# A chunked DeltaNet with a SiLU feed-forward: readout rows of even and odd heads exchanged, recurrence steps paired anew across the quarters of TensorE

## The chip, the cores and the metric

The kernel runs on one core of a Trainium2 chip. A core has five engines that run their own instruction queues side by side: TensorE (PE, matrix products from SBUF into PSUM), VectorE (DVE), ScalarE (ACT), GpSimd (POOL) and SyncE (SP, which here issues nearly all DMAs). The metric is the device time of one execution in microseconds.

PSUM has eight banks, and the kernel divides them into three rooms: three banks for room A, three for room CC, two for room M. A product of small matrices uses a part of TensorE's array: the rows of the array belong to the partitions that its operands lie on, the columns to the partitions that its result goes to. A product with 64 partitions on either side uses one quarter of the array. Write LO for partitions 0 to 63 and HI for 64 to 127. The quarters (from LO to LO) and (from HI to HI) are the main diagonal; (LO to HI) and (HI to LO) are the other diagonal.

## The reference

For 4 batches and 8 heads, over 768 tokens of width 48, a state of 48 x 48 numbers per head is carried from token to token; the output of all heads of a token, side by side, is a row of 384 numbers, which a feed-forward layer takes on.

```python
k_n = k / (np.linalg.norm(k, axis=-1, keepdims=True) + 1e-06)
for t in range(S):
    y[:, :, t] = np.einsum('bhd,bhde->bhe', q[:, :, t], state)
    v_old = np.einsum('bhde,bhd->bhe', state, k_n[:, :, t])
    state = state + beta_t * np.einsum('bhd,bhe->bhde', k_n[:, :, t], v[:, :, t] - v_old)
x = y.transpose(0, 2, 1, 3).reshape(4 * 768, 8 * 48)
h = x @ w_in                 # 384 -> 2048
out = (h * sigmoid(h)) @ w_out   # 2048 -> 384
```

Everything is float32, except that the feed-forward weights arrive as pairs of 32-bit words and are narrowed on the chip.

## The kernel before

The 768 tokens are cut into six chunks of 128 (`c` from 0 to 5), each of two halves of 64 (`hf`). Inside a half the recurrence over tokens is solved at once with the inverse of a triangular 64 x 64 matrix per head, so that only the states go from half to half. The batches form two groups of two (`g`), and each group has 16 heads (2 batches `u`, 4 pairs `p`, and `e`, 0 for the even head of a pair and 1 for the odd one).

`prepare(c)` makes the products of keys with keys and of queries with keys, `invert(c)` inverts the 32 x 32 blocks of the triangular matrices on VectorE and sends them through DRAM to where they are wanted, and `solve(c)` is the recurrence. Its steps are short groups of small products:

- `merge(c, g, second)` (L651) makes the lower left 32 x 32 blocks of the inverses out of the diagonal ones, 32 products of 32 x 32; the second pass multiplies what the first has left in `y`. ACT copies one half of the result (L659, L656) and DVE the other (L660, L657), one behind the other.
- `keys(c, g, hf)` (L676) is what the state gives for the keys, 16 products of 48 x 64 by 48; DVE adds it to `vf` (L681).
- `inner(c, g, hf)` (L688) multiplies `vf` by the inverse, 16 products; ACT copies the result to `zbuf` (L454).
- `update(c, g, hf)` (L708) makes the change of the state out of `zbuf`, 16 products; DVE adds it to the state (L713).
- `old(c, g, hf)` (L749) and `new(c, g, hf)` (L762), 16 products each, add into one PSUM bank the readout of the queries from the state and from `zbuf`. ACT copies the odd heads' rows to `part` (L770), from which five DMAs on SP's queue put them where they belong in `xT`; ACT and DVE in turn copy the even heads' rows straight into `xT` (L454, L457).

Each of these 16 products lies on one quarter, and even and odd heads use the two quarters of one diagonal: with `hf` 0, all of them the main diagonal; with `hf` 1, `keys`, `update` and `new` the other diagonal, `inner` and `old` the main one.

`together(a, b)` issues one product of `a`, one of `b`, and so on in turn. `made(c, g, hf)` is `update` and behind it `new`. The feed-forward is `hidden` (L848: `phid`, full-array products with 256 columns, whose SiLU ACT makes) and, from chunk 1 on, `combine` (L945: chains of full-array products with 192 columns, over sums that DVE makes, `sum_g`, L928). It is cut into pieces, and the loop over the chunks sets by hand how many pieces stand behind each step of the recurrence (`run(n)`), and how many of the squares and norms of the next chunk's keys are issued with them (`go(long, n)`; POOL squares, L328, DVE adds, L332, and the norm steps L346 to L373). The pieces next to a recurrence step come from the chunk before; from the seventh step on `hidden` of the same chunk begins, which reads `xT`.

`pin` keeps the order on each engine as it is written. TensorE's queue is therefore one line of recurrence steps and feed-forward pieces in turn.

Of the kernel before, what the change touches and what calls it, by code (L numbers as in the profile page):

```python
# [21 lines left out]
def kernel(  # L22
# [10 lines left out]
    nc = tc.nc  # L33
    B, H, S, D = q.shape
    DM, DFF = moe_w_in.shape
    P = 128
# [600 lines left out]
    def merge(c, g, second):  # L637

        if c not in ys:
            ys[c] = work.tile([P, 2, HH, T], FP32, name="y", tag="g", bufs=1)  # L640
        y = ys[c]
        pm = bank(A, "px" if second else "py")
        for n in range(HH):
            for k in range(2):
                even, odd = slice(W * k, W * k + T), slice(W * k + T, W * (k + 1))
                if second:
                    to, left, right = even, y[odd, g, n, :], xis[g][odd, n, T:W]
                else:
                    left = aps[c, g][even, 0, n // H, n % H, T:W]
                    to, right = odd, xes[c][even, g * HH + n, :]  # L650
                pin(nc.tensor.matmul(  # L651
                    pm[to, T * n : T * (n + 1)], lhsT=left, rhs=right, start=True, stop=True
                ))
        pm = pm[:].rearrange("p (h t) -> p h t", h=HH)
        if second:
            pin(nc.scalar.copy(xis[g][0:T, :, T:W], pm[0:T]))  # L656
            pin(nc.vector.tensor_copy(out=xis[g][W : W + T, :, T:W], in_=pm[W : W + T]))  # L657
        else:
            pin(nc.scalar.copy(y[T:W, g], pm[T:W]))  # L659
            pin(nc.vector.tensor_copy(out=y[W + T : P, g], in_=pm[W + T : P]))  # L660

    def of_heads():

        for u in range(HB):
            for p in range(NP):
                for e in range(2):
                    yield u, p, e, u * NP + p, slice(W * e, W * e + D), HALVES[e]
# [4 lines left out]
    def keys(c, g, hf):  # L672

        ph = bank(CC, "ph")
        for u, p, e, n, of, _ in of_heads():
            yield pin(nc.tensor.matmul(  # L676
                ph[on(e, hf), n * D : (n + 1) * D], lhsT=kqs[c, g * HB + u][of, p, 0, on(e, hf)],
                rhs=states[g][of, u, p, 0:D], start=True, stop=True,
            ))
        to = vfs[c][:, hf, g * HB : (g + 1) * HB]  # L680
        pin(nc.vector.tensor_tensor(out=to, in0=to, in1=by_heads(ph), op=ALU.add))  # L681
# [19 lines left out]
    def update(c, g, hf):  # L701

        if c == NCH - 1 and hf == 1:
            return
        pu = bank(CC, "pu")
        for u, p, e, n, _, to in of_heads():
            rows = on(e, hf)
            yield pin(nc.tensor.matmul(  # L708
                pu[to, n * D : (n + 1) * D], lhsT=kbufs[c % 2][rows, g * HB + u, p, e, :],
                rhs=zbuf[rows, g * HB + u, hf, p, 0:D], start=True, stop=True,  # L710
            ))
        to = states[g][:, :, :, 0:D]
        pin(nc.vector.tensor_tensor(out=to, in0=to, in1=by_heads(pu), op=ALU.add))  # L713
# [31 lines left out]
    def old(c, g, hf):  # L745

        py = pys[g] = bank(A, "pyc")
        for u, p, e, _, of, to in of_heads():
            yield pin(nc.tensor.matmul(  # L749
                py[to, C * p + W * u : C * p + W * (u + 1)],  # L750
                lhsT=states[g][of, u, p, :], rhs=kqs[c, g * HB + u][of, p, 1, on(e, hf)],
                start=p == 0 and u == 0, stop=False, skip_group_check=True,
            ))
        if hf == 1:
            by_act(read[:], py[:, 0 : 512 : W])

    def new(c, g, hf):

        py = pys.pop(g)
        for u, p, e, _, _, to in of_heads():  # L760
            rows = on(e, hf)
            yield pin(nc.tensor.matmul(  # L762
                py[to, C * p + W * u : C * p + W * (u + 1)], lhsT=zbuf[rows, g * HB + u, hf, p, :],
                rhs=aps[c, g][rows, 1, u, 2 * p + e, :], start=False, stop=True, skip_group_check=True,
            ))
        xT, half = x_half(c, g, hf)
        if g == 0:
            parts[c, hf] = work.tile([P, 2, NP, C], FP32, name="part", tag="x", bufs=1)
        part = parts[c, hf][:, g]
        pin(nc.scalar.copy(part[W : W + D], py[W : W + D].rearrange("p (a t) -> p a t", a=NP)))  # L770
        turns = 0
        for h in chained(range(1, H, 2), range(0, H, 2)):
            f = D * h
            while f < D * (h + 1):
                n, at = min(D * (h + 1) - f, P - f % P), W * (h % 2) + f - D * h
                while h % 2 == 0 and (n > T and at % W or f % P % W and n > T):
                    n = T
                to = xT[f % P : f % P + n, f // P, half]
                if h % 2 == 1:
                    in_line(nc.sync.dma_start(out=to, in_=part[at : at + n, h // 2, :]))  # L780
                else:
                    (by_dve if turns % 2 else by_act)(to, py[at : at + n, C * (h // 2) : C * (h // 2 + 1)])
                    turns += 1
                f += n

    def made(c, g, hf):

        together(update(c, g, hf))
        together(new(c, g, hf))
        if hf == 1 and g == 1:  # L790
            load_q(c + 1)

    def solve(c):

        if c == 0:
            merge(0, 0, False)
            merge(0, 1, False)
            yield
            merge(0, 0, True)
            merge(0, 1, True)  # L800
            yield
            together(inner(0, 0, 0, CC))
            together(inner(0, 1, 0, M))
            yield
            first_outputs(0)
            yield
            first_outputs(1)
            yield
            together(update(0, 0, 0), update(0, 1, 0))
            yield  # L810
            together(keys(0, 0, 1))
            yield
        else:
            for second in (False, True):
                for g in range(2):
                    merge(c, g, second)
                yield
            together(keys(c, 0, 0))
            yield
            together(keys(c, 1, 0), inner(c, 0, 0))  # L820
            yield
            together(inner(c, 1, 0), old(c, 0, 0))
            made(c, 0, 0)
            yield
# [406 lines left out]
    go(long, 99)  # L1231
    load_v(1)
# [82 lines left out]
```

## Time and profile before

| | |
|---|---|
| time, median of 3 runs | 743.81 us (740.95 to 746.01) |
| profiled execution | 745.45 us |
| its span, first to last instruction | 743.7 us |
| mean granted TensorE clock | 0.973 |
| PE busy | 713.0 us, 96% |
| DVE busy | 392.7 us, 53% |
| ACT busy | 204.5 us, 27% |
| POOL busy | 82.1 us, 11% |
| DMA queue 1 | 47.63 MB, 32.6% of 16 engines |

The profile lists instructions by source line, engine and tile. `L688 PE MATMUL pz<-vf,xi 64*64 64x48` is a product issued at line 688 that writes tile `pz`, on a part of the array with 64 rows and 64 columns, with 64 x 48 moving numbers; each product of the program stands in it as two records. PE's records overlap, as products are pipelined, so that a step's time is read from its first start to the start of what comes next. The page cuts the span into 40 slices, and gives in tenths how busy each engine was and what clock TensorE was granted; the same can be asked for any stretch of time. A chunk takes some 111 us, and its recurrence about 40 us of them, feed-forward pieces included.

### The profile page before, as it was taken

The numbers are of one execution on the slowest core, as the hardware profiler recorded it, in microseconds if no ns is written. First come the engines' busy times: TensorE is split into PE (matmuls) and PEld (weight loads), VectorE is DVE, ScalarE is ACT, GpSimd is POOL, SyncE is SP. The second block draws the span as 40 slices with busy tenths as digits, with TensorE's granted clock in tenths as the row PEclk, the third lists the DMA queues.
The fourth block names the chain that finished last, engine by engine and source line by source line (L and its number), as shares of the span: only waits on it lengthen the run. The fifth ranks groups of instructions, "written<-read, shape, count | busy, mean of one in ns | idle before, by whom it ended". The sixth has DMA issues, their size and how long they took to land. (4 is left out here: it accounts for less than half of the span.)

```text
span 743.7 us, 21255 instructions
## 1 busy us (share of the span) xinstructions
PE 713.0 (96%) x9416; PEld 616.8 (83%) x9416; DVE 392.7 (53%) x930; ACT 204.5 (27%) x429; POOL 82.1 (11%) x86
## 2 busy tenths in 40 slices
PE   7869988899989999999999999999999999999996
PEld 5557875486778989988989988989988989989996
DVE  5755588995442693542693542693543692321112
ACT  3523556122223113223113223113223113231120
POOL 4041426300002000002000001000001000000000
PEclk9865999999999999999999999999999999999999
DMA  8754368404017504017404017504017104010000
GB/s 121 210 119 130 130 147 204 74 5 97 11 27 100 86 22 87 8 40 100 86 22 86 10 43 96 86 22 86 10 45 95 42 22 87 11 36 1 22 0 22
DMA packets 149132, 49.25 MB, mean 66 GB/s; under 512 B 134881, under 2 KB 142177, under 8 KB 149041
## 3 DMA queue, kind: packets, MB, share of 16 engines
q1 hardware_dynamic: 146928, 47.63, 32.6%
q8 instruction: 74, 1.21, 0.7%
q10 hardware_dynamic: 2112, 0.26, 0.3%
q14 instruction: 18, 0.14, 0.1%
HBM read 33.91 MB, written 11.80 MB: 61 GB/s over the span
## 5 line engine op out<-in xcount | busy, mean ns | idle before, releaser
L848 PE MATMUL phid<-xT,w_in 128*128 128x256 f32 x1152 | 263.6, 383 | 2.8 <-DVE n L361 0.7
L848 PEld LDWEIGHTS phid<-xT,w_in 128*128 128x128 f32 x1152 | 214.0, 190 | 37.0 <-DVE o L953 2.9
L858 ACT ACTIVATE gT<-phid 128x512 f32<-128x512 f32 x96 | 57.3, 597 | 179.4 <-PE phid L848 163.5
L514 DVE SCALAR_TENSOR_TENSOR rank<-g,step,x 128x31 f32<-128x31 f32 (+15 forms) x155 | 62.2, 402 | 14.3 <-DMA g<-blocks 9.8
L928 DVE TENSOR_TENSOR sums_of_g<-gT 128x384 f32<-128x384 f32 (+1 forms) x60 | 29.3, 510 | 68.2 <-ACT gT L858 57.8
L519 DVE TENSOR_TENSOR x<-x,rank 128x31 f32<-128x31 f32 (+15 forms) x155 | 54.7, 353 | 5.8
L945 PE MATMUL px<-sums_of_w,sums_of_g 128*128 128x192 f32 x320 | 57.2, 330 | 0.0
L945 PE MATMUL py<-w_out,sums_of_g 128*128 128x192 f32 x320 | 56.9, 329 | 0.0
L945 PEld LDWEIGHTS px<-sums_of_w,sums_of_g 128*128 128x128 f32 x320 | 52.0, 190 | 0.8
L945 PEld LDWEIGHTS py<-w_out,sums_of_g 128*128 128x128 f32 x320 | 52.2, 190 | 0.5 <-issue 0.2
L878 PE MATMUL po<-w_out,gT 128*128 128x384 f32 x128 | 45.5, 498 | 2.9 <-POOL w_out L199 2.9
L328 POOL TENSOR_TENSOR sq<-kb 128x384 f32<-128x384 f32 x24 | 19.5, 835 | 237.6 <-PE px L651 219.3
L688 PEld LDWEIGHTS pz<-vf,xi 64*64 64x64 f32 x768 | 41.0, 144 | 5.2 <-issue 2.9
L688 PE MATMUL pz<-vf,xi 64*64 64x48 f32 x768 | 43.9, 227 | 0.3
L457 DVE COPY xT<-pyc 32x128 f32<-32x128 f32 (+2 forms) x66 | 18.7, 284 | 47.3 <-ACT xT L454 47.3
L449 DVE TENSOR_TENSOR ap<-pa,above 128x256 f32<-128x256 f32 x40 | 15.1, 420 | 50.9 <-ACT ap L454 39.0
L878 PEld LDWEIGHTS po<-w_out,gT 128*128 128x128 f32 x128 | 23.1, 189 | 19.8 <-POOL w_out L199 6.0
L749 PE MATMUL pyc<-kq,state 48*64 48x64 f32 x704 | 36.3, 227 | 0.0
L749 PEld LDWEIGHTS pyc<-kq,state 48*64 48x64 f32 x704 | 33.3, 138 | 3.4 <-issue 3.4
L439 PE MATMUL pa<-kq 48*64 48x128 f32 (+1 forms) x896 | 27.6, 264 | 4.9 <-ACT kq L423 4.6
L713 DVE TENSOR_TENSOR state<-state,pu 128x384 f32<-128x384 f32 x22 | 12.1, 553 | 36.3 <-PE pu L708 36.2
L439 PEld LDWEIGHTS pa<-kq 48*64 48x64 f32 x896 | 21.9, 136 | 11.1 <-ACT kq L423 6.5
(159 smaller groups left out, 920.0 us busy)
## 6 DMA issues: line engine op xcount, KB each, us to landing
vf<-in_v_dram SPq DMA_DIRECT2D x24, 192.0 KB, 5.3
out_dram<-o SPq DMA_DIRECT2D x48, 96.0 KB, 2.2
sums_of_w<-in_moe_w_out_dram SPq DMA_DIRECT2D x5, 768.0 KB, 6.2
w_out<-in_moe_w_in_dram SPq DMA_DIRECT2D x4, 768.0 KB, 4.7
blocks<-ap SPq DMA_DIRECT2D x44, 64.0 KB, 1.9
g<-blocks SPq DMA_DIRECT2D x5, 512.0 KB, 3.7
up<-x SPq DMA_DIRECT2D x5, 512.0 KB, 4.0
xi<-up SPq DMA_DIRECT2D x40, 64.0 KB, 2.6
```

The costliest lines, as they stand in the source:

```text
L328: pin(nc.gpsimd.tensor_tensor(out=squared[c, b // HB][:, b % HB], in0=kb, in1=kb, op=ALU.mult))
L439: pin(nc.tensor.matmul(pa[e][half, p * n * W : (p + 1) * n * W], lhsT=kq[rows, p, 0, half], rhs=kq[rows, p, js[0] : js[-1] + 1, half], sta ...
L457: return pin(nc.vector.tensor_copy(out=to, in_=of))
L514: pin(nc.vector.scalar_tensor_tensor(out=tv, in0=g[:, 0:m, m : m + 1].to_broadcast([P, m, n]), scalar=step[:, m : m + 1], in1=x[:, m : m + ...
L519: yield pin(nc.vector.tensor_tensor(out=x[:, 0:m, m:T], in0=x[:, 0:m, m:T], in1=tv, op=ALU.add))
L688: yield pin(nc.tensor.matmul(pz[rows, n * D : (n + 1) * D], lhsT=xis[g][rows, u * H + 2 * p + e, :], rhs=vfs[c][rows, hf, g * HB + u, p, : ...
L749: yield pin(nc.tensor.matmul(py[to, C * p + W * u : C * p + W * (u + 1)], lhsT=states[g][of, u, p, :], rhs=kqs[c, g * HB + u][of, p, 1, on ...
L848: pin(nc.tensor.matmul(ph[:, j * GT : (j + 1) * GT], lhsT=w_in[:, a, (2 * f + j) * P : (2 * f + j + 1) * P], rhs=xTs[c, hf][:, a, :], star ...
L858: pin(nc.scalar.activation(out=gTs[f // FG][:, f % FG, :], in_=ph[:], func=ACTF.Silu, scale=0.5))
L878: pin(nc.tensor.matmul(po[n][:, 0:DM], lhsT=gTs[f // 2 // FG][:, f // 2 % FG, at : at + C], rhs=w_outs[f // HFF][:, f % HFF, :], start=(f ...
L928: pin(nc.vector.tensor_tensor(out=sums_of_g[:, k, fs], in0=of[0], in1=of[1], op=op))
L945: pin(nc.tensor.matmul(to, lhsT=at, rhs=quarter(f, *b) if isinstance(b, tuple) else sums_of_w[b][:, f], start=start and f == 0, stop=f == ...
```

## The change

Three things change.

1. `old` and `new` put the even heads' readout on the upper half of the PSUM bank and the odd heads' on the lower half, where it was the other way round. Both products so move to the other diagonal than before. The copies and DMAs that take the bank's rows to `xT` follow.
2. `merge` becomes a generator that yields before each pair of products, so that it can be issued in turn with another step.
3. In chunks 1 to 5 the steps of `solve` are paired anew, twelve steps in place of nine; `made` issues `update` and `new` in turn. In chunk 0 the second half of the steps changes in the same way. The loops that place feed-forward pieces and norm steps behind the recurrence steps are counted anew.

```diff
@@ merge
         for n in range(HH):
             for k in range(2):
+                if k == 0:
+                    yield
@@ old (and new in the same way)
-                py[to, C * p + W * u : C * p + W * (u + 1)],
+                py[HALVES[1 - e], C * p + W * u : C * p + W * (u + 1)],
@@ new
-        pin(nc.scalar.copy(part[W : W + D], py[W : W + D].rearrange("p (a t) -> p a t", a=NP)))
+        pin(nc.scalar.copy(part[0:D], py[0:D].rearrange("p (a t) -> p a t", a=NP)))
@@ made
-        together(update(c, g, hf))
-        together(new(c, g, hf))
+        together(update(c, g, hf), new(c, g, hf))
@@ solve, chunks 1 to 5
-            for second in (False, True):
-                for g in range(2):
-                    merge(c, g, second)
-                yield
-            together(keys(c, 0, 0))
-            yield
-            together(keys(c, 1, 0), inner(c, 0, 0))
-            yield
-            together(inner(c, 1, 0), old(c, 0, 0))
+            together(merge(c, 0, False))
+            yield
+            together(merge(c, 1, False), merge(c, 0, True))
+            yield
+            together(merge(c, 1, True), keys(c, 0, 0))
+            yield
+            together(keys(c, 1, 0), old(c, 0, 0))
+            yield
+            together(inner(c, 0, 0), old(c, 1, 0))
+            yield
             made(c, 0, 0)
             yield
-            together(old(c, 1, 0), keys(c, 0, 1))
+            together(inner(c, 1, 0), keys(c, 0, 1))
+            yield
             made(c, 1, 0)
             yield
@@ solve, all chunks
-        together(keys(c, 1, 1), inner(c, 0, 1))
-        yield
-        together(inner(c, 1, 1), old(c, 0, 1))
+        together(inner(c, 0, 1), keys(c, 1, 1), old(c, 0, 1))
+        yield
+        together(inner(c, 1, 1), old(c, 1, 1))
+        yield
         made(c, 0, 1)
         yield
-        together(old(c, 1, 1))
         made(c, 1, 1)
         yield
@@ chunk 0
-    for n in range(5):
+    for n in range(6):
         go(solving)
-        run(2)
+        run((2, 1, 1, 2, 2, 2)[n])
...
-        fill(2)
-        go(long, (0, 1, 1, 4, 6)[n])
+        fill((2, 2, 2, 2, 1, 1)[n])
+        go(long, (0, 1, 1, 4, 3, 3)[n])
@@ chunks 1 to 5
-        for n in range(6):
+        for n in range(8):
             go(solving)
-            run(2 if n in (2, 3) else 1)
-            if n >= 2:
+            run(2 if n == 7 else 1)
+            if n >= 3:
                 go(long, 4)
...
-        for n in range(3):
+        for n in range(4):
             go(solving)
             run()
```

The numbers of instructions of each kind, and of DMAs, stay the same.

More of the change, by code (lines that the diff above doesn't have):

```diff
@@ L747, in old @@
         py = pys[g] = bank(A, "pyc")
-        for u, p, e, _, of, to in of_heads():
+        for u, p, e, _, of, _ in of_heads():
             yield pin(nc.tensor.matmul(
-                py[to, C * p + W * u : C * p + W * (u + 1)],
+                py[HALVES[1 - e], C * p + W * u : C * p + W * (u + 1)],
                 lhsT=states[g][of, u, p, :], rhs=kqs[c, g * HB + u][of, p, 1, on(e, hf)],
@@ L759, in new @@
         py = pys.pop(g)
-        for u, p, e, _, _, to in of_heads():
+        for u, p, e, _, _, _ in of_heads():
             rows = on(e, hf)
             yield pin(nc.tensor.matmul(
-                py[to, C * p + W * u : C * p + W * (u + 1)], lhsT=zbuf[rows, g * HB + u, hf, p, :],
+                py[HALVES[1 - e], C * p + W * u : C * p + W * (u + 1)], lhsT=zbuf[rows, g * HB + u, hf, p, :],
                 rhs=aps[c, g][rows, 1, u, 2 * p + e, :], start=False, stop=True, skip_group_check=True,
@@ L774, in new @@
             while f < D * (h + 1):
-                n, at = min(D * (h + 1) - f, P - f % P), W * (h % 2) + f - D * h
+                n, at = min(D * (h + 1) - f, P - f % P), W * (1 - h % 2) + f - D * h
                 while h % 2 == 0 and (n > T and at % W or f % P % W and n > T):
@@ L795, in solve @@
         if c == 0:
-            merge(0, 0, False)
-            merge(0, 1, False)
-            yield
-            merge(0, 0, True)
-            merge(0, 1, True)
-            yield
+            for second in (False, True):
+                for g in range(2):
+                    together(merge(0, g, second))
+                yield
             together(inner(0, 0, 0, CC))
```

## The prediction

> **What bounds the kernel now.** I read the page's parts 1 and 2 first, then who TensorE waits for, then its order of time in one chunk.
>
> ```profile
> span 743.7 us, 21255 instructions
> ...
> PE 713.0 (96%) x9416; PEld 616.8 (83%) x9416; DVE 392.7 (53%) x930; ACT 204.5 (27%) x429; POOL 82.1 (11%) x86
> ...
> PEclk9865999999999999999999999999999999999999
> ```
>
> TensorE (PE) is busy almost throughout; no other engine is near it. From 100 to 660 us its waits add up to some 11 us; the longest two groups are below (us in total, times, longest), both in the first quarter.
>
> ```profile
> PE po L878 <- POOL w_out L199: 2.9, 5, 0.7
> PE pt L413 <- DMA z<-in_q_dram: 2.4, 2, 2.1
> ```
>
> So from chunk 1 on the time is what PE spends, and an edit is worth the PE time it removes. Chunk 2's recurrence runs from 289.9 to 329.1 us. Its order of time (start, length, group; a product of the program stands as two records):
>
> ```profile
> 289.89 2.21 PE L651 MATMUL py<-xe,ap 32*32 32x32 f32 x128
> 292.03 1.57 PE L945 MATMUL py<-w_out,sums_of_g 128*128 128x192 f32 x8
> 293.53 2.21 PE L651 MATMUL px<-xi,y 32*32 32x32 f32 x128
> 295.67 1.57 PE L945 MATMUL py<-w_out,sums_of_g 128*128 128x192 f32 x8
> 297.17 1.14 PE L676 MATMUL ph<-state,kq 48*64 48x48 f32 x32
> ```
>
> ```profile
> 307.78 1.13 PE L708 MATMUL pu<-z,kb 64*64 64x48 f32 x32
> 308.70 1.16 PE L762 MATMUL pyc<-ap,z 64*64 64x64 f32 x32
> 309.79 1.57 PE L945 MATMUL px<-sums_of_w,sums_of_g 128*128 128x192 f32 x8
> 311.29 0.27 PE L749 MATMUL pyc<-kq,state 48*64 48x64 f32 x1
> ...
> 312.27 1.09 PE L708 MATMUL pu<-z,kb 64*64 64x48 f32 x32
> ```
>
> Lengths overlap, so I count from start to start.
>
> **Rates.** One diagonal (two quarters): 32 `pu` records take 308.70 - 307.78 = 0.92 us, 29 ns each; `pyc<-ap,z`, with 64 columns, 1.09. Both diagonals: `old` and `keys(1,0,1)`, 64 records from 311.29 to 312.27, 0.98 us, 15 ns each. Before the change `keys(1,0,0)` with `inner(0,0)`, both on one diagonal, take 301.03 to 303.06, 2.03 us. So a pair that moves onto both diagonals halves. For 32x32 tiles, 128 records on two tiles take 2.14 us; four tiles at once are seen at 33.10 to 34.29 (L584, 128 records, 1.19 us), though with 16 columns, not 32.
>
> **Chunk 2 before.** The nine recurrence steps, start to the next wide group: 2.14, 2.14, 1.07, 2.03, 3.93, 2.95, 1.07, 3.78, 2.78 = 21.9 us.
>
> **After, without the last merge.** Four pairs (`keys`+`old`, `inner`+`old` twice, `inner`+`keys`) at 1.08 = 4.3. Four `update`+`new` at 1.17 (set by `new`: 1.09 and a remainder) = 4.7; before they took 0.92 + 1.09 each. The step of three has one product on the main diagonal and two on the other: 64 records there at 30 ns, 2.1. `merge(0,F)` alone 1.1; `merge(1,F)` with `merge(0,T)`, four tiles, 1.15. Together 13.35.
>
> **The last merge with `keys(0,0)`: the term that decides.** In the rebuilt order each of the 16 `keys` products (64x64) alternates with two 32x32 products, on the same quarters. Nothing overlaps, so at the least it costs both parts as now, 2.1 us. The trace has no change between 32x32 and 64x64; the nearest rows are changes to and from the full array:
>
> ```profile
> 300.78 0.33 PE L945 MATMUL px<-sums_of_w,sums_of_g 128*128 128x192 f32 x1
> 301.03 0.33 PE L676 MATMUL ph<-state,kq 48*64 48x48 f32 x4
> ```
>
> A 128x192 product normally follows in 0.163 us (2.60 for 16 in the chain); here 0.255, so 0.09 more. It is 0.09 at all full-clock changes without a wait, to 32x32 and 64x64 alike. From the last small record to the first wide one it is 0.121 (32x32) and 0.148 (64x64), where records of one quarter follow in 0.03 and 0.06. If 32 to 64 costs the same, a round is 0.121 + 0.094 (the first pair of records after a change) + 0.148 + 0.059 (four merge records) = 0.42 us, and 16 rounds 6.75 us. I take 6.75, the end all nearby rows point to; the other end, 2.1, stays for a rival.
>
> The Trainium skill, TensorEngine Tiling (Array Packing), section Key Properties, says that a change of tiling mode drains TensorE, and speaks against this step. By that rule it is 6.75 too; no row here shows 32 against 64.
>
> **Other terms per chunk.** Three more steps, so three more pairs of changes: +0.28 (0.09 each; the other half is in the step lengths). Waits: DVE now has `S4` (1.36 us), four `add_squares` that wait for POOL (its second pair starts only after the first is summed) and the first norm steps ahead of the state's addition (0.55); counted in us from the end of the last merge, DVE is through with `vf` at 2.0 and 3.0, `S4` at 4.4, the squares at 7.7, the norm steps at 8.75, the state at 9.3. `keys(0,1)` wants it at 8.9, so +0.4, and all PE work queues behind. `merge(0,T)` wants `y` 1.5 us after its products, and the ACT copy (0.58) and DVE copy (0.70) in turn need 1.6: +0.1. A present wait of 0.17 at 320.9 goes. Waits in all +0.35 net, bounds 0 and 1. The readout copies and DMAs only exchange rows: same counts, same queue order on SP; `xT`'s last DMA landed 5.0 us after `made(1,0)`, and the first `phid` still comes 4.9 after.
>
> Sum without the clock: 13.35 + 6.75 + 0.28 + 0.35 - 21.9 = -1.2, say **-1.1 us** a chunk. Chunk 5 has no second update to pair: -0.6. Chunk 1 waits 2.4 us for `xT` at 204 to 208 now, about 1.1 less when a longer step stands ahead: -2.2. Chunk 0 changes only its second half, 8.7 us of steps to 5.7; much of that is lost to the DMA and narrowing waits above: -1 (0 to -3). Chunks 2 to 4 give -3.3; in all -3.3 - 2.2 - 0.6 - 1 = **-7 us**.
>
> **The clock.** The granted clock is full from 71.8 us on but for one stretch (columns: sum, busy time and records of PE, PEld, DVE, ACT, POOL, clock, DMA):
>
> ```profile
> 204.87:208.28 3.41, 1.64 (x6) 0.89 (x6) 3.17 (x13) 0.39 (x1) 0.00 (x0) 1.00 0.20 48
> 208.28:211.69 3.41, 3.41 (x56) 2.87 (x56) 0.27 (x1) 0.00 (x0) 0.00 (x0) 0.50 0.13 32
> 54.68:58.09 3.41, 3.41 (x105) 3.05 (x100) 1.90 (x4) 1.15 (x2) 0.62 (x1) 0.50 0.05 16
> ```
>
> One sparse stretch of 3.41 us is followed by 3.41 us at half clock; and 3.41 us filled with 32x32 products leave it at half. The stretches of one clock in the trace last 3.41, 6.83, 10.24 or more: multiples of 3.41. A step of 6.75 us in which records stream for a third of the time at most (0.04 or 0.027 us each of six in a round of 0.42), on a corner of the array, holds one such stretch whole. Price: on average 1.7 us of the step are left when the clock drops, and the changes at half clock are 1.4 to 1.6 times as long (0.166 and 0.242 us, at 57 to 75 us), +0.9; afterwards it stays low to the end of the first well filled stretch. If that means three quarters full (my assumption), and the step ends anywhere in one, that is 1.3 stretches or 4.3 us at half speed, +2.2. So +3.1 a chunk, bounds 1.7 (one stretch) and 5.1 (three). While PE is slow the 0.35 of waits go. Five chunks: 15.5 - 1.75 = +14. With -7: **+7 us**.
>
> The profiled execution took 745.45 us (span 743.7 and 1.7 around it), 1.6 over the median 743.81; I add the difference to the median: **751 us**.
>
> **Rivals.**
> - *The changes cost, the clock holds.* Then -7: 737 us. For it: the stretch from 290.20 holds mostly 32x32 products and keeps full clock. Against: those were dense; here two thirds is gaps.
> - *32 and 64 change for nothing.* The step costs 2.1, the clock has no cause to drop: -7 - 5 x 4.65 = -30, 714 us. For it: no row shows this change, and 48x64 with 64x64 mix freely. Against: 0.09 at every change that is seen, whatever the sizes. This is the other side.
> - *The diagonals don't interleave for `update`+`new`* (64 rows against the 48 of the pair seen): four steps back at 2.0, +3.4 in each of five chunks, 768 us. Little speaks for it: `keys`+`inner` already mix 48 and 64 rows at 15 ns. Chance 0.03.
> - *A product held up on its quarter holds up all behind it.* In the step of three, two products in a row use one quarter: four records at 59 ns for each of 16 such pairs, 3.8 us against 2.1, +1.7 in six chunks, 761 us. Against: by it `keys`+`inner` at 301 us, built alike, would take 3.8, and takes 2.03; the later `keys` product of the other quarter starts 14 ns behind the first, 0.1 us ahead of the `inner` product between them. Chance 0.02.
>
> The Trainium skill, TensorE: Matmul & The Clock Gate, section The mechanism (Part 3), has this last one as its rule: matmuls start strictly in program order. The trace disagrees, with the 14 ns.
>
> **How the numbers follow.** Forecast 0.60 (745 to 764: the clock's bounds), clock holds 0.20, free change 0.15, the last two 0.05. The range leaves out the free change and the tails: 733 to 764. A measurement of this kernel (740.95 to 746.01) tells about 1% from no change: below 736.4 lie the free change and under half of the holding clock, 0.24; above 751.2 half of the forecast and the last two, with the tail of the waits, 0.38; between, 0.38.
>
> **What would show it.** In the profile after: `px`/`ph` alternating for 6 to 8 us in each of chunks 1 to 5, against 2.1; the clock at 0.50 behind each; pairs of 64 records in about 1 us, the step of three in 2.1; PE waiting for the DVE `state` addition. I am wrong if that step takes under 3 us, or the clock stays at 1.00 through it.

## The result

The changed kernel takes 755.31 us (median of 4 runs, 754.84 to 755.62). The kernel before took 743.21 us beside it (4 runs, 740.95 to 746.01). The ratio is 1.016, with a 95% interval of 1.012 to 1.020. The change makes the kernel slower by 12 us; the forecast was 751 us, 7 us slower.

### The profile page after: what moved, and what is told of

It is laid out like the page before. It is cut to its first block, busy times and chain, and to the rows that moved or that the text cites. A ratio compares the mean times of both kernels' runs of the same rounds, so it can differ in the third digit from the quotient of the medians.

```text
span 753.8 us, 21237 instructions
## 1 busy us (share of the span) xinstructions
PE 722.1 (96%) x9416; PEld 611.3 (81%) x9416; DVE 393.4 (52%) x930; ACT 204.8 (27%) x429; POOL 82.6 (11%) x86
## 3 DMA queue, kind: packets, MB, share of 16 engines
q8 instruction: 74, 1.21, 0.6%
## 4 chain that ended last, share of the span: by engine, by line
PE 74%; DVE 13%; DMA 7%; issue 2%; ACT 2%; SPq 1%; POOL 0%; DVEq 0%; POOLq 0%; ACTq 0%
PE phid L849 26%; PE px L946 11%; PE py L946 9%; PE ph L678 4%; DVE rank L514 4%; DVE x L519 4%; PE px L653 3%; PE pa L439 3%; DMA z<-in_q_dram 3%; PE pz L690 3%; PE pw L295 3%; PE pt L413 3%; PE pu L710 2%; PE py L653 2%; PE po L879 2%
## 5 line engine op out<-in xcount | busy, mean ns | idle before, releaser
L849 PEld LDWEIGHTS phid<-xT,w_in 128*128 128x128 f32 x1152 | 213.6, 190 | 36.5 <-issue 4.9
L946 PE MATMUL px<-sums_of_w,sums_of_g 128*128 128x192 f32 x320 | 63.7, 352 | 0.0
L946 PEld LDWEIGHTS px<-sums_of_w,sums_of_g 128*128 128x128 f32 x320 | 56.5, 204 | 0.9
L678 PE MATMUL ph<-state,kq 48*64 48x48 f32 x704 | 56.1, 243 | 0.0
L879 PE MATMUL po<-w_out,gT 128*128 128x384 f32 x128 | 47.4, 512 | 2.9 <-POOL w_out L199 2.9
L678 PEld LDWEIGHTS ph<-state,kq 48*64 48x64 f32 x704 | 42.9, 153 | 8.3 <-issue 4.3
L449 DVE TENSOR_TENSOR ap<-pa,above 128x256 f32<-128x256 f32 x40 | 15.1, 420 | 56.3 <-ACT ap L454 42.8
L690 PEld LDWEIGHTS pz<-vf,xi 64*64 64x64 f32 x768 | 32.1, 146 | 8.4 <-issue 5.9
L690 PE MATMUL pz<-vf,xi 64*64 64x48 f32 x768 | 35.1, 235 | 0.0
L751 PE MATMUL pyc<-kq,state 48*64 48x64 f32 x704 | 34.6, 244 | 0.0
L946 PE MATMUL py<-w_out,gT 128*128 128x192 f32 x160 | 33.2, 362 | 0.0
L653 PE MATMUL px<-xi,y 32*32 32x32 f32 x768 | 32.5, 211 | 0.6 <-issue 0.6
```

The costliest lines, as they stand in the source:

```text
L653: pin(nc.tensor.matmul(pm[to, T * n : T * (n + 1)], lhsT=left, rhs=right, start=True, stop=True))
L678: yield pin(nc.tensor.matmul(ph[on(e, hf), n * D : (n + 1) * D], lhsT=kqs[c, g * HB + u][of, p, 0, on(e, hf)], rhs=states[g][of, u, p, 0:D ...
L690: yield pin(nc.tensor.matmul(pz[rows, n * D : (n + 1) * D], lhsT=xis[g][rows, u * H + 2 * p + e, :], rhs=vfs[c][rows, hf, g * HB + u, p, : ...
L751: yield pin(nc.tensor.matmul(py[HALVES[1 - e], C * p + W * u : C * p + W * (u + 1)], lhsT=states[g][of, u, p, :], rhs=kqs[c, g * HB + u][o ...
L849: pin(nc.tensor.matmul(ph[:, j * GT : (j + 1) * GT], lhsT=w_in[:, a, (2 * f + j) * P : (2 * f + j + 1) * P], rhs=xTs[c, hf][:, a, :], star ...
L879: pin(nc.tensor.matmul(po[n][:, 0:DM], lhsT=gTs[f // 2 // FG][:, f // 2 % FG, at : at + C], rhs=w_outs[f // HFF][:, f % HFF, :], start=(f ...
```

## The profile after

The page of the changed kernel, the three lines that answer to those of before:

```profile
span 753.8 us, 21237 instructions
...
PE 722.1 (96%) x9416; PEld 611.3 (81%) x9416; DVE 393.4 (52%) x930; ACT 204.8 (27%) x429; POOL 82.6 (11%) x86
...
PEclk9957999998999998899999799999899999699999
```

PE has the same 9,416 records and is busy for 9 us more, at the same 96%. So the loss is not waiting: PE's waits from 100 to 660 us rose from 11.0 to 15.1 us only. The clock line tells more: before, one row of nines from slice 5 on; now five dents at even distances, one per chunk. The two groups of waits that were shown of before (us in total, times, longest):

```profile
PE pt L413 <- DMA z<-in_q_dram: 6.5, 4, 3.5
PE po L879 <- POOL w_out L199: 2.9, 5, 0.7
```

The wait for the next chunk's queries grew from 2.4 to 6.5 us; it comes back below. Now chunk 2 in order of time (start, length, group), at the step that mixes `keys(0,0)` with the last merge:

```profile
290.73 0.31 PE L678 MATMUL ph<-state,kq 48*64 48x48 f32 x2
290.97 0.25 PE L653 MATMUL px<-xi,y 32*32 32x32 f32 x4
291.15 0.31 PE L678 MATMUL ph<-state,kq 48*64 48x48 f32 x2
291.39 0.25 PE L653 MATMUL px<-xi,y 32*32 32x32 f32 x4
```

A round of one `keys` product and one merge pair takes 291.15 - 290.73 = 0.42 us. It repeats 16 times, and the step lasts from 290.73 to 298.93, 8.20 us, where the two parts one behind the other took 2.1 us of PE before. PE counts as busy all through it. The same stretch by the clock (columns: sum, busy time and records of PE, PEld, DVE, ACT, POOL, granted clock, DMA share, GB/s):

```profile
287.50:290.91 3.41, 3.41 (x142) 2.92 (x140) 1.43 (x3) 1.48 (x3) 0.00 (x0) 1.00 0.36 57
290.91:294.33 3.42, 3.42 (x50) 2.62 (x49) 1.79 (x4) 0.00 (x0) 0.00 (x0) 1.00 0.02 5
294.33:297.74 3.41, 3.41 (x37) 2.56 (x35) 0.00 (x0) 0.00 (x0) 0.00 (x0) 0.50 0.00 0
...
304.57:307.98 3.41, 3.41 (x59) 2.97 (x61) 2.47 (x6) 0.00 (x0) 1.26 (x2) 0.50 0.00 0
307.98:311.39 3.41, 3.41 (x98) 3.05 (x92) 2.07 (x8) 1.18 (x3) 0.35 (x1) 1.00 0.02 5
```

The stretch from 290.91 lies wholly inside the step: PE "busy" 3.42 of 3.42 us (a record counts as busy to its end, which the profile models), with only 50 small records in it. The next one runs at half clock, and full clock comes back at 307.98, well after the step. In chunks 1 to 5 the low clock lasts 6.83, 13.65, 10.24, 6.83 and 13.65 us, 51.2 in all: two to four stretches of 3.41.

The paired steps, on the other hand, do interleave. The three-way step starts like this, `inner` products of the main diagonal and `keys` products of the other in turn, and lasts 2.07 us for 96 records; every pair on both diagonals of chunk 2 takes 1.08 or 1.09 us where the clock is full, `update` with `new` too.

```profile
318.83 0.25 PE L690 MATMUL pz<-vf,xi 64*64 64x48 f32 x1
318.84 0.25 PE L678 MATMUL ph<-state,kq 48*64 48x48 f32 x1
318.85 0.25 PE L690 MATMUL pz<-vf,xi 64*64 64x48 f32 x1
...
318.98 0.22 PE L690 MATMUL pz<-vf,xi 64*64 64x48 f32 x1
318.99 0.25 PE L751 MATMUL pyc<-kq,state 48*64 48x64 f32 x2
```

The first `old` product stands third in the program's order, on the quarter that the first `keys` product uses; its records start only at 318.99, behind five records of `inner` products.

Below, "recurrence" is the time from a chunk's first merge product to its last `new` product, summed over chunks 1 to 5 of the profiled execution: 198.0 us before, 213.6 after.

## The experiments

**1. Take the mix apart, or thin it out.** The theory: the loss is the mixed step alone, by the changes of tile size and the clock. The first three kernels change nothing but the turns of this step.

```diff
@@ e1_apart, solve
-            together(merge(c, 1, True), keys(c, 0, 0))
+            together(merge(c, 1, True))
+            together(keys(c, 0, 0))
@@ b2_blocks (in b4_blocks: 4 rounds, with 4 and 4)
+            pair = merge(c, 1, True), keys(c, 0, 0)
+            go(pair[0])
+            for _ in range(8):
+                go(pair[1], 2)
+                go(pair[0], 2)
+            for part in pair:
+                go(part)
```

> The changed kernel, but in chunks 1 to 5 the last merge and keys(0,0) stand one behind the other, in place of one product of the one, one pair of the other in turn; they stay in the same step, and nothing else moves. Theory (32x32 and 64x64 products that alternate on the same quarters cost 0.09 us at every change, and the gaps let the clock drop): the step falls from 8.2 us to 2.2, the clock stays full in chunks 1 to 5, and the time is 717 us (715 to 724, where DVE's state addition is waited for again). Rival one (the loss lies elsewhere: other new pairs, the waits for DMAs, the longer list of steps): 743 or more. Rival two (the changes cost, but the clock drops for another reason): the step falls to 2.2, half clock stays in each chunk, 730 to 738.

> The changed kernel, but the last merge and keys(0,0) take turns in blocks: two keys products, then two pairs of merge products, eight rounds in place of sixteen. Theory (0.42 us for a round of one, and 0.07 us more for the second product and pair in it, so 0.49): the step takes 3.9 us, and as the stretches of the clock are 3.41 us long it drops in none to three of five chunks: 720 to 734. Rival (the cost goes with the number of products, not of changes): the step stays near 7 to 8 us and the time near 750.

> As the kernel with blocks of two, but blocks of four: four rounds. Theory: a round is 0.21 us for its two changes and 0.09 us for each keys product with its merge pair, so the step takes 2.4 to 2.9 us, the clock does not drop, 718 to 724. Rival (the cost goes with the number of products): near 750.

Measured, beside a kernel before of 746.56 us: apart 718.69 us (ratio 0.963, 0.960 to 0.966), blocks of two 736.29 (0.987, 0.982 to 0.992), blocks of four 723.30 (0.970, 0.967 to 0.973). The page of the kernel with the two apart, and the step in its order of time:

```profile
span 716.9 us, 21240 instructions
...
PEclk9956999999999999999999999999999999999999
```

```profile
286.00 0.59 PE L653 MATMUL px<-xi,y 32*32 32x32 f32 x25
287.16 0.82 PE L653 MATMUL px<-xi,y 32*32 32x32 f32 x39 [0.57 <-issue]
287.91 1.14 PE L678 MATMUL ph<-state,kq 48*64 48x48 f32 x32
```

The dents are gone, and the step takes 2.2 to 3.0 us. That one line of `solve` was worth 37 to 39 us (ratios 1.016 and 0.963). With eight rounds the step takes 3.93 us in chunks 1 to 3, 0.492 a round, as worked out (4.18 and 4.38 in the last two); with four rounds 2.94 in three chunks, 0.735 a round, the upper end (3.16 and 3.30 in the other two). With blocks of two the clock dropped behind this step in chunks 3 and 4 and inside it in chunk 5; with blocks of four in none of the five. The 736.29 us lie 2 us above the range that was expected of blocks of two, the other two times inside theirs. Rivals one (the loss lies elsewhere) and two (the clock drops for another reason) fall with the first run, and the cost goes with the number of changes, not of products: the products are the same 48 in all four kernels.

**2. Is it the shared quarters?** In the mixed step both parts use the main diagonal. This kernel mixes the merge with a step that uses the other quarters.

```diff
@@ q_other_quarters, solve
-            together(merge(c, 1, True), keys(c, 0, 0))
+            together(merge(c, 1, True), old(c, 0, 0))
             yield
-            together(keys(c, 1, 0), old(c, 0, 0))
+            together(keys(c, 0, 0), keys(c, 1, 0))
```

> The changed kernel, but the last merge (32x32 tiles on the main diagonal) takes turns with old(0,0) (64x64 on the other diagonal, so no quarter is shared), and then keys(0,0) and keys(1,0) take turns with each other, both on one diagonal, 2.0 us. Theory A (a change of tile size costs wherever the tiles lie): the mixed step takes 7 to 8 us, the clock drops in each of chunks 1 to 5, and with the 1.0 us more for the two keys the time is 755 to 765. Theory B (only tiles that share a quarter wait for each other): the mixed step takes 1.1 to 2.2 us, the clock stays full, 717 to 728.

Measured: 767.04 us, ratio 1.028 (1.023 to 1.034), 2 us above what theory A gave. The start of the mixed step:

```profile
293.17 0.33 PE L751 MATMUL pyc<-kq,state 48*64 48x64 f32 x2
293.42 0.25 PE L653 MATMUL px<-xi,y 32*32 32x32 f32 x4
293.61 0.32 PE L751 MATMUL pyc<-kq,state 48*64 48x64 f32 x2
```

A round takes 0.435 us against 0.422 with shared quarters (`old` has 64 columns to `keys`' 48), and the clock drops in all five chunks. The step takes 7.98 us in chunk 2. Theory A holds: not the quarter but the change of tile size costs. Nor does it cost to take turns as such: `keys` with `inner`, which alternate on one diagonal before the change, take 2.03 us for 64 records, where 32 of one step alone take 0.92 to 1.09. The Trainium skill, TensorEngine Tiling (Array Packing), section Key Properties, says that a change of mode drains TensorE while a change of tile alone does not; both halves of that sentence agree with these runs, the first with 0.43 us a round, the second with the 1.08 us of pairs on both diagonals.

**3. The price of the clock by itself.** Two kernels keep all 16 rounds but put wide products among them.

```diff
@@ h_wide_between, solve: yields after 5 and after 10 rounds, none behind the step
+            for n in range(16):
+                if n in (5, 10):
+                    yield
+                for part in pair:
+                    go(part)
@@ its loop: one piece behind each of nine steps
-        for n in range(8):
+        for n in range(9):
             go(solving)
-            run(2 if n == 7 else 1)
-            if n >= 3:
+            run()
+            if n >= 4:
@@ h2_busy_between, solve
+            for n, _ in enumerate(zip_longest(merge(c, 1, True), keys(c, 0, 0))):
+                if n in (4, 8, 12):
+                    busy(2)
```

> The changed kernel with the same 16 rounds of keys(0,0) and the last merge, but two of the feed-forward pieces that stand behind other steps are put among the rounds (after 5 and after 10 of them), so that the wide products come in between; the next step follows the last rounds without a piece. No work is added. It tells the price of the changes from the price of the clock. Theory (both cost): the clock stays full in chunks 1 to 5, the rounds still take 0.42 us each, 6.8 us in all beside the pieces, and the time falls by the 10 to 14 us that the low clock cost, to 741 to 748, or 0.99 to 1.00 of the kernel before (a wait of up to 1.3 us for DVE's state addition may come, as one piece less stands ahead of the step of three). Rival one (the low clock cost next to nothing, the changes all): 755, as the changed kernel. Rival two (the low clock cost nearly all): 720 to 725.

Measured: 756.80 us (three runs, 755.58 to 758.73; a fourth took 767.23), ratio 1.015 (1.013 to 1.018), no better than the changed kernel. The expectation failed, but not towards rival one, because its condition was not met: the clock still fell in four of the five chunks of the profiled execution. (That is the fourth run. The other three had a mean granted clock of 0.960 to 0.963, where the profiled one had 0.948 and the next kernel, whose clock holds, has 0.976 to 0.979; so theirs fell too, though less.) Two stretches of it, columns as above:

```profile
412.92:416.33 3.41, 3.41 (x40) 2.66 (x39) 2.71 (x6) 0.06 (x1) 0.00 (x0) 1.00 0.00 0
300.28:303.70 3.42, 3.42 (x39) 2.74 (x37) 1.55 (x4) 0.33 (x1) 0.00 (x0) 1.00 0.03 5
```

The first was followed by half clock, the second by full clock; by busy time and records they are the same. What differs is how much of a feed-forward piece the stretch holds; the last section returns to it. In chunk 2 the clock held, and there the rounds took 2.35 + 2.11 + 3.38 - 1.08 = 6.76 us.

> The changed kernel, but after every four of the sixteen rounds of keys(0,0) and the last merge stand two full-array products of 384 columns whose result nobody reads (work added, nothing moved): 3 times 1.3 us and 0.2 us for the changes around them, 4.5 us in each of chunks 1 to 5, 22.5 in all. So no stretch of 3.41 us holds sparse records alone. Theory (sparse stretches pull the clock down, and that cost 3.3 us a chunk): the clock stays full in chunks 1 to 5, a round still takes 0.42 us, and the time is only 3 to 9 us above the changed kernel: a ratio to the kernel before of 1.020 to 1.030. Rival (the low clock costs nothing, or drops for another reason and stays): 22 us above the changed kernel, a ratio of 1.045.

Measured: 757.93 us, ratio 1.019 (1.015 to 1.023), with 22 us of products added. The page and the order of time:

```profile
span 757.1 us, 21357 instructions
...
PEclk9957999999999999999999999999999999999999
```

```profile
295.30 0.31 PE L678 MATMUL ph<-state,kq 48*64 48x48 f32 x2
295.54 1.56 PE L295 MATMUL pw<-state,ident 128*128 128x384 f32 x4
```

This time the clock is full through the recurrence of all five chunks. In chunk 2 the mixed step takes 293.62 to 304.82, 11.20 us, of which the three wide groups are 4.46 and the rounds 6.74. The recurrence is 213.8 us; without the added groups (5 x 4.46) it is 191.5. The changed kernel needs 213.6 with the same rounds. So the low clock cost 22 us, 4.4 in a chunk (the 51.2 us of low clock, half of them lost, set the upper end at 25.6), and the changes themselves 191.5 less the 172.6 of the kernel with the two apart, 19 us or 3.8 in a chunk. Both are real, and of like size; 22 us of idle work in the right place cost almost nothing.

**4. The mix alone, the rows alone, the order alone.** The kernel before with only the mix; the kernel before with only the rows exchanged; the kernel with the two apart with the rows put back.

```diff
@@ bm_mix_alone, on the kernel before (merge as a generator)
-            for second in (False, True):
-                for g in range(2):
-                    merge(c, g, second)
-                yield
-            together(keys(c, 0, 0))
+            for g in range(2):
+                together(merge(c, g, False))
+            yield
+            together(merge(c, 0, True))
+            yield
+            together(merge(c, 1, True), keys(c, 0, 0))
@@ n1_rows_back, on the kernel with the two apart; x0_rows_alone: the reverse, on the kernel before
-                py[HALVES[1 - e], C * p + W * u : C * p + W * (u + 1)],
+                py[HALVES[e], C * p + W * u : C * p + W * (u + 1)],
...
-        pin(nc.scalar.copy(part[0:D], py[0:D].rearrange("p (a t) -> p a t", a=NP)))
+        pin(nc.scalar.copy(part[W : W + D], py[W : W + D].rearrange("p (a t) -> p a t", a=NP)))
```

> The kernel before, with the one edit that keys(0,0) and the last merge take turns in chunks 1 to 5; no rows are exchanged and no other step is moved. Theory: the two take 6.8 us and more in place of 2.1, and the clock drops behind them in each of the five chunks, so 36 to 40 us more than the kernel before, a ratio of 1.048 to 1.054. Rival (the cost comes of the mix together with the new order around it): under 1.03.

> The kernel with the last merge and keys(0,0) apart, but the readout's rows are put back: old and new lie on the diagonals of before, everything else stays. It tells what the diagonals bring from what the new order brings. Theory (a pair on one diagonal takes 2.0 us, on both 1.08): three pairs with old lose 0.95 us each and four update+new 0.9 each, 6.4 us in each of chunks 1 to 5 and 4 in chunk 0, so 36 us more than with the rows exchanged: 755, or 1.01 of the kernel before; the step of three stays at 2.1. Rival (the gain came from the order and the shorter waits, whatever the diagonals): within 10 us of the kernel with the two apart, 718 to 729.

> The kernel before with the readout's rows exchanged and nothing else: the order of the steps is that of before. Theory (the rows bring something only where the order puts the two diagonals beside each other): inner(1,0)+old(0,0) and inner(1,1)+old(0,1) halve, 0.95 us each, old(1,0)+keys(0,1) comes to lie on one diagonal and loses 1.0; update and new stand one behind the other as before. So -0.9 us in a chunk and in chunk 0, a ratio of 0.991 to 0.995. Rival (the rows bring the gain by themselves, through the copies or the DMAs): 0.96 to 0.98.

Measured: the mix alone 785.51 us beside 745.81, ratio 1.054 (1.052 to 1.056), 40 us: the cost belongs to the mix and not to the order around it. Order without the rows: 748.85 us, 1.004 (1.003 to 1.006). Rows without the order: 734.05 us beside 744.25, 0.986 (0.982 to 0.990). Both together, with the mix apart: 0.963.

With the rows put back, each of the seven pairs that the exchange serves takes 2.00 to 2.06 us in chunk 2 in place of 1.09, and the step of three 2.00, as expected, and the recurrence of chunks 1 to 5 grows by 204.2 - 172.6 = 31.6 us, where 32 were worked out. The sum came out at 30 us against 36 in all the same: the stretches behind the recurrence are 3.6 us shorter, as the slower steps cover some of the waits for the queries, and the first merge of chunk 0 starts 3.8 us earlier (50.8 against 54.6), which no edit explains.

The rows alone bring 10 us, which is more than the 0.9 us a chunk that I gave them and outside the expected ratio. In chunk 2 the four steps that change take 2.77, 3.54, 2.88 and 2.77 us where the kernel before takes 3.93, 2.95, 3.78 and 2.77: 1.5 us less, not 0.9. The start times say why. With the rows exchanged, `update`'s last record starts at 304.38 us and `new`'s first at 304.21, 0.17 us ahead of it; in the kernel before the two start at 308.69 and 308.70. A step on the other diagonal starts before the one ahead of it has issued its last record, though nothing alternates them; I had counted only the pairs that alternate. The exchange makes three more such seams in a chunk, at some 0.2 us each: the first of the four steps gains 1.16 us in place of 0.95, and the second, with two of them, loses 0.59 in place of 1.0. Over the five chunks the recurrence is 7.9 us shorter. Of the rest, 1.5 us lie ahead of chunk 1, where no step of chunk 0 got shorter by more than 0.02 us with the clock full; no edit explains them.

**5. What pulls the clock down?** The kernel before, with the first merge's products issued three times over.

```diff
@@ d_dense_small, merge
-        for n in range(HH):
+        for n in list(range(HH)) * (1 if second or c == 0 else 3):
```

> The kernel before with the first merge's 32x32 products issued three times over in chunks 1 to 5 (the same results again), 6.4 us of records that follow one another at full density on two tiles of 32x32, in place of 2.1. That adds 4.28 us a chunk, 21.4 in all. It asks what pulls the clock down. Theory one (it is the share of the array and of the time that streams: over all full-clock stretches of 3.41 us seen so far those under 0.25 were followed by half clock and those over 0.33 were not; a dense stream on two 32x32 tiles comes to 0.10): half clock behind this step in each of the five chunks, 2 to 4 us more each, a ratio of 1.042 to 1.056 to the kernel before. Theory two (it is the gaps between the records): no gap, no drop, a ratio of 1.027 to 1.031.

Measured: 791.25 us beside 744.25, ratio 1.064 (1.058 to 1.069), above both theories, with half clock behind the step in all five chunks. The stretch ahead of the drop in chunk 2, and one with a like busy time in the kernel with the two apart that was followed by full clock:

```profile
299.75:303.17 3.42, 2.53 (x158) 2.41 (x153) 0.70 (x1) 0.58 (x1) 0.00 (x0) 1.00 0.03 6
```

```profile
286.70:290.11 3.41, 2.95 (x78) 2.85 (x79) 2.52 (x5) 0.57 (x1) 1.61 (x2) 1.00 0.02 5
```

The drop fits theory one. But the experiment is not clean: the long step was not free of gaps. In each chunk two or three gaps of 0.2 to 1.6 us stand between its records, waits for which the profile names no releaser ("issue", 6.9 us in all from 100 to 660 us), so that the stretch above is busy for 2.53 us of 3.42. Of the 42 us by which the profiled execution (786.61 us) lies above the kernel before, the gaps of all five chunks are 8; the other 34 lie where theory one expected the sum (31 to 42). Whether a step without any gap would drop the clock stays open.

**6. A kernel that beats both.** With the two apart, two waits are left that an order can mend. The first attempt moved the queries' load behind the first half's readout, which was a mistake of mine: the queries are loaded into `zbuf`, and the second half's `inner` still writes there. In this kernel part of the next chunk's queries is therefore overwritten, and the readout of chunks 2 to 5 is made of other numbers.

```diff
@@ best_apart and best2_apart, on the kernel with the two apart
-            together(merge(c, 1, True))
             together(keys(c, 0, 0))
+            together(merge(c, 1, True))
@@ best_apart, made
-        if hf == 1 and g == 1:
+        if hf == (c == 0) and g == 1:
             load_q(c + 1)
@@ best2_apart: the load moves from the end of made to new, ahead of its DMAs
+        if hf == 1 and g == 1:
+            load_q(c + 1)
         turns = 0
```

> The kernel with the last merge and keys(0,0) apart, with two more edits: keys(0,0) stands ahead of the last merge, so that the merge's wait for the copies of y (0.7 us in the longest chunk) is covered by 1.1 us of products; and the next chunk's queries are loaded after the first half's readout, not after the second's, so that TensorE's waits for that DMA (5.3 us in all from 100 to 660 us) go. Theory: 711 to 715 where the kernel without the two takes 718.7, or 0.953 to 0.958 of the kernel before. Rival (the waits only move to the next thing that is late, xT's DMAs among them): 716 to 720.

Measured: 742.56 us, ratio 0.996 (0.994 to 0.999), far above the 711 to 715 expected. The load does come early, but ACT's copy into `zbuf` then has to wait for it, and TensorE for that copy:

```profile
ACT z L454 <- DMA z<-in_q_dram: 35.5, 4, 9.0
```

```profile
PE pyc L751 <- ACT z L454: 17.3, 4, 5.2
```

The clock falls to half at each of these four waits as well, for 3.41 or 6.83 us.

> The kernel with the last merge and keys(0,0) apart, with two more edits: keys(0,0) stands ahead of the last merge, so that the merge's wait of 0.7 us for the copies of y is covered; and the loads of the next chunk's queries stand on SP's queue ahead of the last five readout DMAs, not behind them. Theory: the first wait goes, 0.5 us in three or more chunks, and of TensorE's 5.3 us of waits for the queries at least half: 713 to 716 on the scale on which the kernel without the two took 718.7 and the kernel before 746.6, a ratio of 0.955 to 0.960. Rival (something else is late next, the scores' copies or xT): 0.961 to 0.966.

Measured: 711.25 us beside 744.25, ratio 0.956 (0.952 to 0.960), as expected. The wait for the queries has left the list of waits from 100 to 660 us, and the clock is full from 122 us to the last 2 us:

```profile
span 708.0 us, 21238 instructions
...
PEclk9965999999999999999999999999999999999999
```

TensorE's waits from 100 to 660 us fall from 17.5 to 9.3 us. Largest now is one wait of 2.7 us for ACT's copy of `kq` (L423). The pause in the merge, which I had put down to the copies of `y`, is gone as well; but in the trace of the kernel with the two apart it comes in the middle of the merge's records, after the 25th of 64, so its cause is not the copies alone and was not settled.

## Why the prediction was right, and by which steps

The forecast was 7 us slower; it is 12 us slower, with the mechanism that was named. Against its own terms (us; the measured ones from the profiled executions):

| term | forecast | measured |
|---|---|---|
| rounds of the mixed step, 16 x 0.42 | 6.75 | 6.74 (with wide groups between, full clock) |
| the changes in chunks 1 to 5, over the two apart | 5 x 4.65 = 23 | 19 |
| low clock in chunks 1 to 5, less the waits that it covers | 14 | 22 |
| all other edits, chunks 1 to 5 (the forecast's sum without the clock, less the 23 of the changes) | -29 | -25 (172.6 - 198.0) |
| chunk 0 | -1 | -6 |
| behind the recurrence | 0 | +0.6 |

- **The bound.** TensorE sets the time before and after; no other engine's share moved by more than a point.
- **The mixed step** was sized from rows of changes to and from the full array, since no row showed 32 against 64. The choice of the upper end, 6.75, was right to 0.01 us, and its two parts fit as well (from a `keys` product to the merge pair behind it 290.97 - 290.73 = 0.24 us, from there to the next 0.18; 0.242 and 0.180 in the sum). Rival "32 and 64 change for nothing" is what the kernel would have been without the mix: I gave it 714 us, 30 less than before, and the kernel with the two apart takes 28 less.
- **The rates.** 1.08 to 1.09 for pairs (`update` with `new` I had at 1.17), 1.21 for four tiles (1.15), 2.07 for the step of three (2.1). (The working under the 2.1 was loose: 64 records at 30 ns are 1.9, and 2.03 is what 64 records on one diagonal took before.) So rivals three and four fall. For the fourth, the Trainium skill, TensorE: Matmul & The Clock Gate, section The mechanism, has matmuls start strictly in program order; the 2.07 us, against the 3.8 that this order would give, disagree, and so do the starts at 318.98 and 318.99 above.
- **The clock.** The mechanism is shown: a sparse stretch, then half clock, in all five chunks, and gone when the mix is taken apart, or when wide products stand in it. The size was too small: I took 1.3 stretches behind the step, from an assumption that a stretch three quarters full is enough to lift it, and saw two to four in all. The 4.4 us lie inside the bounds that I gave (1.7 to 5.1). (The range's upper end, 764, is 2 us more than these bounds give: 743.81 - 7 + 5 x 5.1 = 762.3.)
- **The waits.** DVE's addition to the state did not hold up `keys(0,1)` in chunk 2 of the changed kernel, as PE was slow there; with the two apart that step takes 1.24 us in place of 1.08, so 0.16 where I had 0.4. What I missed is the queries' load: SP issues it behind the readout's DMAs, and with faster steps these stand closer to its due time; it cost 4 us over four chunks (6.5 against 2.4), outside the recurrence. Inside it other waits were missed, and they are most of the 4 us by which "all other edits" fell short: with the two apart, chunks 2, 3 and 4 gained 2.4, 1.0 and 0.8 us less than forecast, and TensorE waits 2.0, 0.7 and 0.8 us there, where it did not wait before. Of these 1.1 us are for `xT`'s DMA in chunk 2, which the forecast had put at nothing.
- **Chunk 0** is, for its size, the term that was most off. The steps of its second half became 3 us shorter as worked out; I then let waits for DMAs and narrowing eat most of that, and they did not. The other 3 us go with the clock of the startup, which was at half until 65.6 us in the trace of the changed kernel and until 71.8 us in that of before; no edit explains that. Some of it is chance: in the seven traces with the changed kernel's chunk 0 the recurrence of chunk 1 starts anywhere from 170.1 to 174.2 us, this one's first of all, and in three with the chunk 0 of before from 174.8 to 176.3.

The misses partly cancel, so that 751 came as near as 4 us is in part luck; that the sum was a loss, and by these two costs, is not: +8 for the clock, +4 for the other edits, -5 for chunk 0, -4 for the changes. With the forecast's 7 that makes 10 us between the two profiled spans; the other 2 us are that the profiled execution of the kernel before (745.45 us) lay that far over its median.

## What to carry to other kernels

Alternate small products only with products of the same tile size: on different quarters they then run side by side at half the time, while every change between 32x32 and 64x64 tiles costs 0.10 to 0.15 us wherever the tiles lie (the rounds of 0.42, 0.49 and 0.74 us less their products), so keep each size together. A step can cost behind itself as well as in itself (of the 22 us of the low clock some 6 fell inside the mixed steps, which took 39.6 us in place of 33.7, and 16 behind them): look at the granted clock in the stretches after a sparse step, and at the records in a stretch, as a busy PE of 100% hides both. When a change has one bad line among good ones, take the lines apart first: here 37 us of gain stood behind one `together`.

## What the runs showed of the hardware that I had not expected

- **The clock went with how much of the array streams, not with how busy PE is.** I counted in every full-clock stretch of 3.41 us from 100 to 700 us, over 13 kernels of this study (all but the first attempt of the sixth experiment; 2,206 stretches, 34 of them followed by half clock), each record with its share of the array (tile rows x columns / 128 x 128) and its moving columns at 0.83 ns each (wide records of 192 columns follow one another in 0.163 us, those of 384 in 0.323); this is an estimate from the records' shapes, and a stretch or two at the bounds below depends on how it is made. Of the stretches under 0.25 of the array's time all 27 were followed by half clock, from 0.25 to 0.33 6 of 16, above that 1 of 2,163. The two stretches of the third experiment come to 0.29 and 0.40. The share of the time in which anything streams parts them less well: of the 64 stretches with 0.45 to 0.60 of it 11 dropped. The Trainium skill, TensorE: Matmul & The Clock Gate, section Why this matters for your kernels, asks for no idle gaps above some 3 us against a drop in the middle of a kernel; the stretch of 290.91 to 294.33 above, busy throughout, shows that this is not enough.
- **The way back is less sharp.** In the same count, with a column at twice the time, half clock followed stretches at half clock up to some 0.75 of the array's time, and full clock others from some 0.5 on.
- **Steps overlap at their seam.** A step on free quarters starts 0.17 us before the last record of the step ahead, without being alternated with it; that is some 0.6 of the 1.5 us a chunk that the rows alone bring.
- **Dense streams of 32x32 records pause.** Some streams of 64 and more of them (in the kernel with the merge apart and in that of the fifth experiment) show pauses of 0.2 to 1.6 us without a releaser; what they wait for was not settled.
